# An attention and maxout kernel: first loads in another order, other first transposes, one store per output tile, score bursts of three

## The chip, the cores and the metric

The kernel runs on 1 core of one Trainium2 chip. The metric is device microseconds (us) of one execution, from the first instruction to the last. Several executions of each kernel are timed, and the median is quoted with all or with the lowest and highest. Two numbers are quoted per kernel: the timed median, and the "span" of its one profiled execution, which comes out about two microseconds shorter (before: 384.99 timed, 382.8 span).

## The reference

```python
# q, k, v: (8 batches, 8 heads, 1152, 64); w1, w2: (512, 1024); w_out: (1024, 512); all float32
q_pool = q.reshape(8, 8, 576, 2, 64).mean(axis=3)            # 576 pooled queries a head
attn   = softmax(q_pool @ k.T / sqrt(64))                    # 576 x 1152 a head
x      = (attn @ v).transpose(0, 2, 1, 3).reshape(4608, 512) # tokens x features
out    = maximum(x @ w1, x @ w2) @ w_out                     # (4608, 512)
```

The kernel computes the second half as relu(x(w1-w2)) w_out + x(w2 w_out). In the profile L582 (before) or L618 (after) is x(w1-w2), called h below; L609 (L645) is the last product, 12 matmuls of 128x512 for an output tile of 128 tokens, called p. In some variants these lines are one to six off.

## The kernel before

The program is put in order on the host, while it is built. `Plan.op` adds an instruction with the names that it reads and writes, and a planned cost. A loop picks what TensorE does next by these planned times; semaphores then keep the order safe whatever the true times are. So each engine runs a fixed list of instructions, and a new planned cost or rank reorders all lists. Work goes by pairs of heads (32 pairs): scores for two heads at once as two 64-row tiles of TensorE, exponentials on ScalarE (128x1024 each, 336 in all), the product with v (AV), and, once the 4 pairs of a batch are done, x is transposed and h and p run between the scores of the next batches. The score steps need another tiling of TensorE (64 rows) than all else (128 rows), so they come in bursts; a "switch" or "transition" below is a change between the two.

These parts matter (cuts marked):

```python
def load_k(i, lo=0, hi=NT):              # first K in two loads, three tiles and six
    ...
def load_q(i):                           # first queries in two loads, one head (64 partitions) each
    ...
def qtrans(i):                           # pooled queries of a pair: 9 transposes of 64 rows x 128 columns
    ...
def xtrans(b):                           # x of batches 1 to 6: five transposes by DMA, issued from SyncE
    ...
def store(lo, s):
    for half in range(2):                # a tile of 128 tokens: two stores of 64 rows
        n0 = lo + half * HP              # HP = 64, QU = 9, SQ = 576, HP * QU = SQ
        b, at = n0 // SQ, n0 % SQ
        if b % 2:
            at = (at - NB) % SQ
        op("SP", lambda e, b=b, u=at // HP, half=half: e.dma_start(
            out[b * SQ:(b + 1) * SQ, :].rearrange("(p u) e -> u p e", u=QU)[u, :, :],
            osb[s][rows(half), :]), r=[f"osb{s}"], dma=f"d_o{s}", cost=0.4)
...
def burst_size():
    done = [b for b in range(B) if ...]
    return 3 if len(done) * SQ - p_end[0] > LAG else 2
...
X_PE = (0, B - 1)                        # x of the first and last batch: transposed by TensorE
rank = {"q": 6, "k": 6, "x": 5, "a": 4, "w": 3, "p": 2, "h": 1}
```

Column n of a batch's queries inside the kernel is not row n of the output: the queries were loaded with 9 neighbouring rows to a partition, so block u of 64 columns holds the rows 0*9+u, 1*9+u, ..., 63*9+u. A tile of 128 tokens is two such blocks, u and u+1. In four tiles the two blocks belong to two neighbouring batches and have the same u. Each store writes 64 rows of 2048 bytes that lie 9 rows apart.

The softmax here doesn't subtract the row's maximum and nothing guards it: scores larger than these inputs give would overflow.

## Time and profile before

| | before |
|---|---|
| median of 3 runs | 384.99 us (383.74 to 385.46) |
| span of the profiled execution | 382.8 us |
| TensorE busy | 363.7 us, 95% |
| ScalarE busy | 316.9 us, 83% |
| first matmul of h, L582 | 65.85 us |
| end of the last matmul | 378.68 us |
| transitions between 64-row and 128-row work | 272, of which 204 after 65 us |

PE is TensorE at matmuls and PEld at weight loads, DVE is VectorE, ACT ScalarE, POOL GpSimd, and SPq the queue of DMAs that SyncE issues, one after the other. PEclk is the clock that TensorE was granted, in tenths of full speed.

The same execution by stretches: to the first matmul, to the first h, to the end of the last matmul, and the rest. The columns are given by the first line.

```profile
core 0: us, PE busy (x) PEld busy (x) DVE busy (x) ACT busy (x) POOL busy (x), PEclk, DMA share, GB/s
0.00:6.70 6.70, 0.00 (x0) 0.00 (x0) 1.50 (x2) 1.56 (x2) 0.97 (x10) 1.00 0.70 184
6.70:65.80 59.10, 51.75 (x837) 32.08 (x838) 31.03 (x58) 55.57 (x63) 40.05 (x30) 1.00 1.11 368
65.80:378.70 312.90, 311.95 (x4180) 178.76 (x4175) 107.00 (x222) 259.77 (x292) 120.96 (x96) 1.00 0.87 208
378.70:382.80 4.10, 0.00 (x0) 0.00 (x0) 0.69 (x1) 0.00 (x0) 0.00 (x0) 1.00 0.40 84
```

Two lines of the waits of this kernel, and three of SyncE's queue near 90 us, for comparison later. The waits give total us, times, and the longest. Names: qp and qpT are the pooled queries and their transpose, kbf and kT the same for K, xnat and xT for x; sps are the banks of memory into which TensorE writes scores (the score banks), fb its other banks.

```profile
PE fb L323 <- DVE qp L297: 6.7, 1, 6.7
POOL qp L297 <- DMA qpT<-qp: 21.3, 13, 4.3
```

```profile
88.33 3.81 SPq L286 DMA_TRANSPOSE kT<-kbf  x1
...
95.59 7.50 SPq L475 DMA_TRANSPOSE xT<-xnat  x5
103.19 1.94 SPq L336 DMA_TRANSPOSE qpT<-qp  x1
```

TensorE starts by waiting 6.7 us for the first pooled queries. The list of waits has no line of TensorE waiting for a DMA at all. GpSimd waits 21.3 us for transposes by DMA to free their source, without harm.

### The profile page before, as it was taken

Reading aid. Unit: us, or ns where it says so; the run is one execution under the profiler, and the core shown is the slowest. Engines: PE = TensorE matmul, PEld = TensorE weight load, DVE = VectorE, ACT = ScalarE, POOL = GpSimd, SP = SyncE. Lnnn points to the kernel's source line nnn. Section 1 sums busy time; section 2 is a strip of 40 time slices with the busy share of each in tenths; the row PEclk is TensorE's granted clock in tenths of the full one; section 3 lists DMA queues with packets and bytes.
Section 4 is the critical chain, followed back from the end, with each engine's and each line's share of the span. In section 5 each row is a group of like instructions: output and inputs, shape, how many; then the busy total and the mean of one; then the engine's idle time right before and its main releaser. Section 6 shows DMA issues by size and latency. Waiting matters only on the chain.

```text
span 382.8 us, 11318 instructions
## 1 busy us (share of the span) xinstructions
PE 363.7 (95%) x5010; PEld 210.8 (55%) x5010; DVE 140.2 (37%) x283; ACT 316.9 (83%) x355; POOL 162.0 (42%) x135
## 2 busy tenths in 40 slices
PE   2787999999999999999999999999999999999995
PEld 1365546555555555455556565555455655667642
DVE  2274934442234223422252224422442244237201
ACT  3998989999999999999999999999899999902210
POOL 1955597665554555555453535545545110000000
PEclk9999999999999999999999999999999999999999
DMA  8999999999989998999799999999899460121144
GB/s 248 405 391 399 392 257 312 331 309 312 225 234 295 273 272 174 309 320 275 142 265 289 319 179 212 286 258 315 200 236 267 94 109 14 29 44 42 29 95 98
DMA packets 93521, 88.58 MB, mean 231 GB/s; under 512 B 66080, under 2 KB 66592, under 8 KB 93472
## 3 DMA queue, kind: packets, MB, share of 16 engines
q1 hardware_dynamic: 93472, 87.86, 89.4%
q8 instruction: 39, 0.64, 0.7%
q14 instruction: 10, 0.08, 0.1%
HBM read 62.91 MB, written 9.44 MB: 189 GB/s over the span
## 4 chain that ended last, share of the span: by engine, by line
PE 85%; DMA 6%; DVE 4%; POOL 2%; issue 1%; SPq 1%; POOLq 0%
PE fb L378 22%; PE fb L609 21%; PE sps L429 18%; PE fb L582 15%; PE sps L609 4%; DMA qraw<-in_q_dram 3%; DMA kraw<-in_k_dram 2%; PE sps L582 2%; DVE wd L519 2%; POOL qp L297 1%; PE fb L547 1%; DVE xnat L390 1%; POOL vE L304 1%; PE fb L489 1%; DVE wo L523 1%
## 5 line engine op out<-in xcount | busy, mean ns | idle before, releaser
L436 ACT ACTIVATE et<-sps 128x1024 bf16<-128x1024 f32 (+1 forms) x336 | 307.8, 1005 | 19.0 <-PE sps L429 17.2
L378 PEld LDWEIGHTS fb<-vE,et 128*128 128x128 bf16 x2880 | 93.4, 97 | 20.9 <-issue 10.9
L378 PE MATMUL fb<-vE,et 128*128 128x65 bf16 x2880 | 101.9, 193 | 0.3
L297 POOL TENSOR_TENSOR qp<-qraw 64x576 bf16<-64x576 f32 x62 | 88.6, 1429 | 30.6 <-DMA qpT<-qp 21.3
L429 PE MATMUL sps<-qpT,kT 64*128 64x512 bf16 (+7 forms) x1152 | 96.9, 289 | 3.0 <-ACT et L436 2.1
L304 POOL TENSOR_SCALAR vE<-vraw 128x1152 bf16<-128x1152 f32 x32 | 36.9, 1152 | 103.2 <-PE fb L378 95.8
L429 PEld LDWEIGHTS sps<-qpT,kT 64*128 64x128 bf16 x1152 | 41.8, 95 | 51.3 <-issue 19.6
L582 PE MATMUL fb<-xT,wd 128*128 128x512 bf16 (+3 forms) x276 | 63.1, 360 | 0.7 <-DVE stage L623 0.7
L609 PE MATMUL fb<-wo,stage 128*128 128x512 bf16 x240 | 62.4, 380 | 0.0
L593 DVE TENSOR_SCALAR stage<-fb 128x512 bf16<-128x512 f32 (+3 forms) x64 | 41.9, 657 | 32.3 <-PE fb L582 32.1
L388 DVE RECIPROCAL rc<-fb 128x5 f32<-128x5 f32 x64 | 12.4, 194 | 112.3 <-PE fb L378 112.3
L273 POOL TENSOR_SCALAR kbf<-kraw 128x1152 bf16<-128x1152 f32 x31 | 36.2, 1167 | 14.6 <-DMA kraw<-in_k_dram 12.5
L582 PEld LDWEIGHTS fb<-xT,wd 128*128 128x128 bf16 x276 | 22.8, 98 | 29.4 <-DVE stage L593 6.3
L623 DVE COPY stage<-fb 128x512 f32<-128x512 f32 x29 | 20.0, 690 | 50.2 <-PE fb L609 49.7
L609 PEld LDWEIGHTS fb<-wo,stage 128*128 128x128 bf16 x240 | 21.1, 97 | 23.3 <-issue 3.3
L390 DVE TENSOR_TENSOR xnat<-fb,rc 128x320 bf16<-128x320 f32 x64 | 31.5, 491 | 2.2
L609 PE MATMUL fb<-w,xT 128*128 128x512 bf16 x120 | 32.1, 380 | 0.0
L609 PEld LDWEIGHTS fb<-w,xT 128*128 128x128 bf16 x120 | 10.3, 98 | 11.7 <-issue 2.0
L589 ACT ACTIVATE stage<-sps 128x256 bf16<-128x256 f32 (+1 forms) x7 | 2.3, 338 | 16.4 <-PE sps L582 16.4
L620 ACT COPY stage<-sps 128x512 f32<-128x512 f32 x3 | 1.8, 585 | 13.8 <-PE sps L609 13.8
L609 PE MATMUL sps<-wo,stage 128*128 128x512 bf16 x48 | 11.3, 379 | 0.0
L582 PE MATMUL sps<-xT,wd 128*128 128x256 bf16 (+2 forms) x76 | 10.3, 275 | 0.0
(40 smaller groups left out, 96.4 us busy)
## 6 DMA issues: line engine op xcount, KB each, us to landing
vraw<-in_v_dram SPq DMA_DIRECT2D x32, 576.0 KB, 7.7
kraw<-in_k_dram SPq DMA_DIRECT2D x31, 576.0 KB, 6.6
qraw<-in_q_dram SPq DMA_DIRECT2D x31, 576.0 KB, 5.8
out_dram<-stage SPq DMA_DIRECT2D x72, 128.0 KB, 2.4
xT<-in_moe_w_dram SPq DMA_DIRECT2D x4, 512.0 KB, 11.9
stage<-in_moe_w_out_dram SPq DMA_DIRECT2D x4, 512.0 KB, 14.2
stage<-in_moe_w_dram SPq DMA_DIRECT2D x4, 512.0 KB, 13.2
qraw<-in_q_dram SPq DMA_DIRECT2D x2, 288.0 KB, 4.1
```

The source lines that it names most:

```text
L273: op("POOL", lambda g: g.tensor_scalar(kbf[s][:, :, :, :].rearrange("p t h d -> p h t d"), kraw[r][:, :, :, :], 1.0, 1.0, ALU.mult, ALU.mu ...
L297: op("DVE" if i == 0 else "POOL", lambda g, half=half, a=a: g.tensor_tensor(qp[s][:, :, half, :], a[:, :, 0, :], a[:, :, 1, :], ALU.add), ...
L304: op("POOL", lambda g: g.tensor_scalar(vE[r][:, :, :, 0:D].rearrange("p t h d -> p h t d"), vraw[r][:, :, :, :], 1.0, 1.0, ALU.mult, ALU.m ...
L378: last = e.matmul(fb[m][:, sb * 66:sb * 66 + 65], et[:, a:a + P], vE[vs][:, t, half, 0:65], start=(t == 0), stop=(t == NT - 1))
L388: dve(lambda e: e.reciprocal(rc[half][:, :], a[:, :, 64:65]), [f"f{m}"], [f"rc{half}"], 0.19)
L390: dve(lambda e: e.tensor_tensor(xnat[xs][:, :, c:c + D], a[:, :, 0:D], rc[half][:, :].unsqueeze(2).to_broadcast([P, NCH + 1, D]), ALU.mult ...
L429: last = e.matmul(sps[r][:, h, col:col + hi - lo], kT[i % 3][rows(h), t, :], qpT[i % 3][rows(h), lo:hi], start=True, stop=True)
L436: op("ACT", lambda e: e.activation(et2[:, :, c:c + z - a], sps[r][:, :, a - g * W:z - g * W], EXP, scale=scale), r=[f"s{r}"], w=keys + [f" ...
L582: return e.matmul(fb[m][:, 0:size], wd[:, ct, ft * P:(ft + 1) * P], xT[:, ct, n0:n1], start=(ct == 0), stop=(ct == NC_ - 1))
L593: dve(lambda e: e.tensor_scalar_max(gT[:, ft, g0:g0 + size], fb[m][:, 0:size], 0.0), [f"f{m}"], w, 0.1 + size / 960.0)
L609: return e.matmul(fb[m][:, :], lhs, rhs, start=(j == 0), stop=(j == NC_ + NF - 1))
L623: dve(lambda e: e.tensor_copy(osb[o][:, :], fb[m][:, :]), [f"f{m}"], [f"osb{o}", f"f{m}"], 0.63)
```

## The change

The intent is to start earlier (loads and pooling), to make TensorE switch less between its tilings, to issue half as many stores, and to shorten the end. The diff is long; this is its core.

```diff
-        def load_k(i, lo=0, hi=NT):
+        def load_k(i):                     # first K: one load
...
-            for half in range(2) if i == 0 else (None,):
+            for lo, hi in zip(Q0, Q0[1:]) if i == 0 else ((0, QU),):   # Q0 = (0, 5, QU): two column parts
...
+        def cast_q0(i, lo, hi):            # pairs 0 and 1 pooled by VectorE on 128 partitions
+            op("DVE", lambda e: e.tensor_tensor(
+                qpf[i][:, lo:hi, :], qraw[i][:, lo:hi, 0, :], qraw[i][:, lo:hi, 1, :], ALU.add), ...
+        def qtrans0(i, lo, hi):            # and transposed as 64x64 blocks on two quadrants
+                for u in range(lo, hi):
+                    for h in range(2):
+                        last = e.transpose(
+                            mb[rows(h), (u - lo) * HP:(u - lo + 1) * HP],
+                            qpf[i][rows(h), u, :], ident[rows(h), rows(h)])
...
-        def store(lo, s):
-            for half in range(2):
-                ...
+        def store(lo, s, c0=0, c1=E, eng="SP"):
+            b, at = lo // SQ, lo % SQ
+            u = at // HP if b % 2 == 0 else (at - NB) // HP
+            if u == QU - 1:
+                to = out[b * SQ:(b + 2) * SQ, c0:c1].rearrange("(b p u) e -> u b p e", b=2, u=QU)[u]
+            else:
+                to = out[b * SQ:(b + 1) * SQ, c0:c1].rearrange("(p u) e -> u p e", u=QU)[u:u + 2]
+            op(eng, lambda e: e.dma_start(to, osb[s][:, c0:c1]), r=[f"osb{s}"],
+               dma=f"d_o{s}" if eng == "SP" else "d_z", cost=0.75 * (c1 - c0) / E)
...                                         # last tile in two parts, 384 and 128 columns:
+                    queue["p"].extend(p_job(p_at[0], tail, *c) for c in ((0, 384), (384, E)))
...
-            return 3 if len(done) * SQ - p_end[0] > LAG else 2
+            return 3 if done else 2
...
+        for kind, i in zip(*[iter("q2k2b2k3v1b0q3c0c3k4c2v2q4c1v3")] * 2):   # loads, weights among them
...
-        rank = {"q": 6, "k": 6, "x": 5, "a": 4, "w": 3, "p": 2, "h": 1}
+        rank = {"q": 6, "k": 6, "x": 5, "h": 5, "a": 4, "w": 3, "p": 1}
```

The cut parts: the first K is cast in three parts by ScalarE and GpSimd; planned costs, and the stall that the plan allows before a burst, are adjusted; VectorE waits for its own earlier results; the stores at the end are issued at once.

## The prediction

> **What bounds the kernel now.** The page's busy table has PE 95% and ACT 83% busy in a 382.8 us span; the chain that ended last is 85% PE. The spacing of the matmul records splits this up. The first matmul starts at 6.7 us. Until 65.8 us, where the first matmul of w1-w2 (L582) runs, PE has only about 46 us of work (scores, AV, transposes, w21), so about 13 us is idle: ACT sets the pace there. Its 128x1024 exponentials follow each other every 903 ns at best, and 58 groups took 56.5 us from 8.91 us, about 4 us over that pace; the stalls are at 11.6 (0.4), 34.2 (1.2, K of a later pair late through the POOL queue) and 48.5 us (0.9, PE waiting for VectorE). From 65.8 to 378.7 us PE is full: I count about 305 us of work, and little of the rest is waiting. In it are some 200 switches between the 64-row score tiles and 128-row work, 95 to 99 ns extra each. The Trainium skill ("TensorEngine Tiling (Array Packing)", Key Properties) says changing the tiling mode drains TensorE; these gaps agree. The tail is 4.1 us: 0.69 us eviction, two store issues of 0.55 us, 2.3 us to landing. The skill ("DMA: Bandwidth & Descriptors") gives about 2.0 us fixed cost; this agrees.
>
> **What the change does.**
> 1. Bursts of three: the static order has 126 score bursts instead of 132, so 252 switches instead of 264. About 1.2 us, mostly given back by extra small transposes. Net PE work 0.7 us less.
> 2. Early loads and VectorE pooling of the second pair. DMA moves about 400 GB/s until 45 us in the timeline, so only order changes. Walking the new order at that rate, each cast lands before its scores are due. The ACT stalls at 34 and 48 us should go, and the first h matmul moves from group 60 to group 59: about 62 us instead of 65.8. Gain 3.5 to 4 us, all on the critical path since PE is full afterwards.
> 3. Head: nearly nothing. K still lands at about 7.2 us (the same bytes lie ahead). One tile's cast is shorter (0.3 against 0.52 us), so the first exponential comes at 8.7 to 8.9 us. But VectorE's order puts pooling of the second pair's queries (0.75 us, waiting for a fourth load at about 8.6 us) ahead of the copies of the remaining K transposes, so I expect a stall of about 0.6 us before the second exponential.
> 4. Tail: the last tile split 384+128 with one store each: eviction 0.3 instead of 0.69, one issue instead of two. About 0.95 us.
> 5. h ahead of p, and the two mixed: fewer 88 ns waits for a PSUM bank. 0.5 us.
> Half as many stores, and waits of VectorE on itself: off the critical path.
>
> **Prediction.** 385.0 - 3.8 (early phase) - 1.0 (tail) - 0.7 (switches, bank waits) = 379.5 us; 376.5 to 382.5 holds it 8 in 10. Faster by over 2%: 0.2; within 2%: 0.78; slower: 0.02.
>
> **What would show it.** First h matmul near 62 us; exponentials at 903 to 920 ns spacing from 11 to 60 us; a gap before the second exponential ended by VectorE; PE last matmul to span end about 3.1 us; PE idle smaller almost only before 65 us; ACT's last exponential several us before 335 us.
>
> **What would make it wrong.** Loads landing more than 2 us later than I walked, which stalls scores in program order; bursts of three faster than ACT empties the banks, which turns switches into waits on exponentials in the middle; PE waits on transposes by DMA under the new order.

## More of the kernel before

The page of the kernel before: the busy table, rows of the 40 slices (one digit is the busy share of a fortieth of the span, in tenths), the chain of work that ended last, and the row of the output stores in the table of DMA issues (count, size, time from issue to landing).

```profile
span 382.8 us, 11318 instructions
PE 363.7 (95%) x5010; PEld 210.8 (55%) x5010; DVE 140.2 (37%) x283; ACT 316.9 (83%) x355; POOL 162.0 (42%) x135
...
PE   2787999999999999999999999999999999999995
...
PEclk9999999999999999999999999999999999999999
DMA  8999999999989998999799999999899460121144
...
PE 85%; DMA 6%; DVE 4%; POOL 2%; issue 1%; SPq 1%; POOLq 0%
...
out_dram<-stage SPq DMA_DIRECT2D x72, 128.0 KB, 2.4
```

TensorE is full from the fifth slice to the end, its clock is granted in full, and it makes 85% of the chain. Note the DMA row too: the 16 DMA engines are nearly always busy until the last fifth. The 72 stores land 2.4 us after issue.

In the third stretch TensorE is busy for 311.95 of 312.90 us. What is left to gain is in the first two stretches and the last, or in TensorE's work itself. And 0.87 is the DMA share of that third stretch: the DMA engines are little of a spare resource there. (The share adds up the times of the packets, which can overlap: it is 1.11 in the second stretch. So it is a rough measure.)

## The result, and the profile after

| | before | after |
|---|---|---|
| median | 385.02 us (4 runs) | 457.79 us; runs 1234.92, 458.83, 455.62, 456.76 |
| ratio, fast runs | | 1.187 (1.180 to 1.193) |

Ratios here and below are the mean time of one kernel's fast runs over that of the other's of the same rounds, so not quite the ratio of the medians quoted; the range is the 95% interval.

A gain of 1.4% was predicted; the kernel became 19% slower. One execution of four, the profiled one, was far slower still. Two different things have to be kept apart, so both pages follow. First the page of the slow execution:

```profile
span 1233.2 us, 11290 instructions
PE 1183.9 (96%) x4982; PEld 555.3 (45%) x5040; DVE 147.8 (12%) x284; ACT 322.4 (26%) x358; POOL 160.8 (13%) x134
...
L618 PE MATMUL fb<-xT,wd 128*128 128x512 bf16 (+3 forms) x274 | 204.9, 973 | 7.4 <-issue 7.4
```

TensorE is busy for 1183.9 us with as many matmuls as ever; the others' busy times are nearly as before. In the trace, matmuls of 512 columns follow each other 840 ns apart (216 ns before) from 10.7 us to the end. TensorE ran at about a quarter of its rate. The record has no event of a granted clock at all for this execution, and the clock is listed as 1.0. This is a state, not the kernel's normal time, so the same kernel was run again unaltered (after_again below): 456.75 us. Its page is the one to compare with before:

```profile
span 454.9 us, 11290 instructions
PE 373.8 (82%) x4982; PEld 216.5 (48%) x5040; DVE 140.8 (31%) x284; ACT 317.2 (70%) x358; POOL 161.3 (35%) x134
...
PE   4989999993997799883997999857994999999900
...
PEclk9999999997998989995998999996997999999965
DMA  8999899998997997999998999998998520011111
...
PE 41%; DMA 22%; ACT 14%; SPq 10%; POOL 4%; issue 3%; DVE 2%; POOLq 0%; ACTq 0%
...
out_dram<-stage SPq DMA_DIRECT2D x35, 256.0 KB
```

Its stretches, with the same columns as before:

```profile
0.00:61.90 61.90, 51.34 (x821) 31.98 (x827) 34.28 (x63) 54.43 (x62) 36.39 (x36) 1.00 0.95 337
61.90:107.00 45.10, 40.89 (x608) 24.03 (x615) 13.70 (x29) 43.14 (x48) 27.26 (x22) 1.00 1.23 289
107.00:432.00 325.00, 281.55 (x3553) 160.44 (x3598) 92.12 (x191) 219.06 (x248) 97.62 (x77) 0.94 0.87 165
432.00:454.90 22.90, 0.00 (x0) 0.00 (x0) 0.69 (x1) 0.59 (x1) 0.00 (x0) 0.57 0.13 49
```

And lines of its waits:

```profile
POOL qp L315 <- DMA qpT<-qp: 123.0, 20, 13.2
...
PE fb L618 <- DMA xT<-xnat: 23.9, 4, 8.4
...
ACT stage L674 <- DMA out_dram<-stage: 14.3, 1, 14.3
```

What the reader is to see:

- Up to the first h the change did what was predicted: 61.9 us against 65.85. ScalarE's idle times of 1.03 and 0.82 us that end at 36.35 and 50.31 us in before are gone, and 59 exponentials start before the first h instead of 61.
- In the third stretch TensorE is busy for 281.55 of 325 us, where it was full before. What it waits for is transposes by DMA: 23.9 us for xT and 9.3 us for kT directly, and through GpSimd, whose wait for DMA transposes grew from 21.3 to 123.0 us, for later pairs' queries and keys.
- The last stretch, 4.1 us before, is 22.9 us, and in it nothing computes but two evictions. Its last two columns are the clue: the DMA share is 0.13, and 2 of 16 engines are 0.125; they move 49 GB/s.
- The row of the stores has no landing time. The page derives it from the count of 16 on a semaphore, and the stores did not count that way (next paragraph).
- The granted clock is 0.94 in the third stretch. In the trace each of the seven half-rate pieces there begins during an idle stretch of TensorE of 2.4 to 8.4 us or less than 2 us after it (TensorE stands from 103.6 to 110.7 us, and one piece lasts from 107.7 to 114.6), so we read it as a consequence of the waits.

The trace records each arrival at a semaphore. In before, 72 stores make 1152 arrivals, 16 each; loads and transposes make 16 each, in all kernels. In after_again, 37 stores (36 tiles, one of them in two parts) make 163. That is 33 x 3 + 4 x 16. The four with 16 are the tiles that lie in two batches, whose access pattern is 128 rows at one step; the other 33 have a pattern of 2 blocks x 64 rows. The Trainium skill ("DMA: Bandwidth & Descriptors", section "Why a DMA increments its semaphore by 16 and not by 1") says how many engines a DMA uses: the largest number up to 16 that divides the slowest dimension, other than 1, of both access patterns; only those engines count on the semaphore, and the issuing sequencer writes the rest. Three arrivals, two engines and the sequencer's one, are what it says for a slowest dimension of 2. This trace agrees.

So the theory: the slice `[u:u+2]` puts a dimension of size 2 outermost, each such store runs on 2 engines of 16, and everything else that needs all 16 engines waits behind them there. The size fits, as an estimate: the stores' packets of 2048 bytes took 84 ns (median, in before_1store below), and 32 such stores x 64 packets an engine x 84 ns are 172 us on each of the two engines. Spread over 16 engines, all 4608 packets are 24 us an engine. With a DMA share of 0.87 in before's third stretch, taken as even over the engines, each has some 40 us to spare (0.13 x 313), not the 150 us more that two of them would need.

The rivals were these. The first came first: the 1233 us suggested that the new 64x64 transposes of the first queries on two quadrants (Q in the texts), or their being the first work of TensorE, bring about a slow TensorE. The second: a store of 256 KB, or one DMA for a tile, is itself the trouble, whatever its engines. The third: the new order, with its ranks and bursts, costs it.

### The profile page after: what moved, and what is told of

Same layout as the page of the kernel before. It is cut to its first block, busy times and chain, and to the rows that moved or that the text cites. A ratio compares the mean times of both kernels' runs of the same rounds, so it can differ in the third digit from the quotient of the medians.

```text
span 1233.2 us, 11290 instructions
## 1 busy us (share of the span) xinstructions
PE 1183.9 (96%) x4982; PEld 555.3 (45%) x5040; DVE 147.8 (12%) x284; ACT 322.4 (26%) x358; POOL 160.8 (13%) x134
## 4 chain that ended last, share of the span: by engine, by line
PE 94%; issue 3%; another core or an unknown queue 1%; DMA 1%; DVE 0%; ACTq 0%; ACT 0%; SPq 0%
PE fb L414 24%; PE sps L467 22%; PE fb L645 21%; PE fb L618 16%; PE sps L645 4%; PE sps L618 2%; PE fb L584 2%; PE fb L384 1%; DMA kraw<-in_k_dram 1%; PE fb L568 1%; PE sps L414 0%; PE fb L526 0%; PE sps L526 0%; PE fb L341 0%
## 5 line engine op out<-in xcount | busy, mean ns | idle before, releaser
L414 PEld LDWEIGHTS fb<-vE,et 128*128 128x128 bf16 x2835 | 294.4, 169 | 70.2 <-issue 60.3
L414 PE MATMUL fb<-vE,et 128*128 128x65 bf16 x2835 | 309.9, 335 | 0.0
L467 PE MATMUL sps<-qpT,kT 64*128 64x512 bf16 (+7 forms) x1152 | 278.1, 691 | 1.9 <-issue 1.5
L618 PE MATMUL fb<-xT,wd 128*128 128x512 bf16 (+3 forms) x274 | 204.9, 973 | 7.4 <-issue 7.4
L645 PE MATMUL fb<-wo,stage 128*128 128x512 bf16 (+1 forms) x202 | 182.6, 1079 | 15.5 <-issue 15.5
L467 PEld LDWEIGHTS sps<-qpT,kT 64*128 64x128 bf16 x1152 | 83.4, 159 | 209.3 <-issue 201.3
L618 PEld LDWEIGHTS fb<-xT,wd 128*128 128x128 bf16 x288 | 51.5, 189 | 133.9 <-issue 120.1
L645 PE MATMUL fb<-w,xT 128*128 128x512 bf16 (+1 forms) x109 | 97.0, 1090 | 3.1 <-issue 1.9
L645 PE MATMUL sps<-wo,stage 128*128 128x512 bf16 (+1 forms) x63 | 49.0, 1036 | 0.7 <-issue 0.7
L618 PE MATMUL sps<-xT,wd 128*128 128x384 bf16 (+3 forms) x64 | 33.2, 767 | 0.5 <-issue 0.5
```

What stands on the lines that cost most here:

```text
L414: last = e.matmul(fb[m][:, sb * 66:sb * 66 + 65], et[:, a:a + P], vE[vs][:, t, half, 0:65], start=(t == 0), stop=(t == NT - 1))
L467: last = e.matmul(sps[r][:, h, col:col + hi - lo], kT[i % 3][rows(h), t, :], qpT[i % 3][rows(h), lo:hi], start=True, stop=True)
L618: return e.matmul(fb[m][:, 0:size], wd[:, ct, ft * P:(ft + 1) * P], xT[:, ct, n0:n1], start=(ct == 0), stop=(ct == NC_ - 1))
L645: return e.matmul(fb[m][:, 0:c1 - c0], lhs, rhs[:, c0:c1], start=(j == 0), stop=(j == NC_ + NF - 1))
```

## The experiments

Two to four kernels at a time ran on one chip, beside runs of the kernel before there ("before" in the tables). Variants of after are named after_..., of before before_..., and s2_... are after with two stores. The letters of theories in the texts are new in each round (Q in s2_rank's is not the Q of the first). Where the order of TensorE's instructions is said to be the same, that was compared instruction by instruction.

### First round: is it the first transposes?

**after_again**: the changed kernel, unaltered.

> The changed kernel, unaltered, to see whether its slowness repeats on this chip and to have a profile of its usual state. Its first profile (1233 us) shows 128-column transposes 210 ns apart and 512-column matmuls 840 ns apart from the start to the end, against 56 and 216 ns in the kernel before: TensorE runs at about a quarter of its rate all the time and no clock event is recorded. Theory Q (the new 64-row x 64-column query transposes, first work of TensorE, put the clock into a throttled state): about 457 us again, part of the run at the quarter rate, granted clock under 1. Theory D (the denser schedule, bursts of three and h before p[...]): about 457 us, with the low rate in the dense middle, not at the start. Theory I (TensorE starts at 4.7 us, then idles 3.8 us until K[...]): about 457 us, slow from the start. Theory C (chance, this chip only): near 380 us in some rounds.

**after_q128**: after, but the first two pairs' queries transposed as before, 64 rows x 128 columns. TensorE's order of work is the same.

```diff
-                    for h in range(2):
-                        last = e.transpose(mb[rows(h), ...], qpf[i][rows(h), u, :], ident[rows(h), rows(h)])
+                    last = e.transpose(mb[:, ...], qp[i][:, u, :, :].rearrange("p h d -> p (h d)"), ident[0:HP, 0:HP])
```

> The changed kernel with one thing undone: the queries of the first two pairs are transposed as 64 rows x 128 columns, as before (VectorE pools each part in two instructions, one for each head, onto 64 partitions). Loads, order on TensorE and everything else are the same; the order is identical apart from the shape of these 36 transposes. Theory Q: 377 to 383 us, clock as in the kernel before (128-column transposes 107 ns apart at first, 56 ns after some 10 us). Theories D and I: still about 457 us, since density and the early start with the idle stretch are unchanged.

**before_q64**: before, with the change's 64x64 transposes for the first two pairs (the opposite edit).

> The kernel before with only the transposes of the queries of its first two pairs made 64 x 64 (two heads on two quadrants, 18 instead of 9 instructions); the order on TensorE is otherwise identical. Theory Q: over 440 us, perhaps 1200 in some runs, low rate from the start. Theories D and I: 384 to 387 us.

**after_warm**: after, with 32 transposes of the 128x128 identity as TensorE's first work.

```diff
+        op("PE", warm, r=["ident"], w=["s2"], ...)    # 32 transposes of ident into an unused score bank
```

> The changed kernel with 32 transposes of the identity, 128 x 128, put before its first query transposes, so that TensorE does not start with 64 x 64 work; it still idles until K lands. Theory Q in the form that 64 x 64 work is bad only as the first work on a cold array: about 380 us. Theory Q in the form that any 64 x 64 work is bad (the second pair has 18 more at 13.7 us): about 457 us or more. Theory I: about 457 us, since the idle stretch from 5.5 to 8.8 us is still there. Theory D: about 457 us.

| run | all runs, us | before, us | ratio |
|---|---|---|---|
| after_again | 455.88 to 458.79 | 384.54 | 1.189 (1.185 to 1.193) |
| after_q128 | 900.3, 460.15, 460.35, 457.01 | 384.54 | 1.194 (1.189 to 1.199) |
| before_q64 | 383.86 to 384.78 | 384.54 | 1.000 (0.998 to 1.001) |
| after_warm | 454.28 to 456.62 | 384.54 | 1.185 (1.182 to 1.188) |

The rival of the first transposes is dead: without those transposes the loss stays, with them before keeps its time, and other first work changes nothing. The slow state came once more, in after_q128, which has no such transposes (898.6 us span, matmuls of 512 columns 621 ns apart, and again no event of a granted clock).

### Second round: the store alone, on an unchanged order

**after_2stores**: after, with only the two 64-row stores back. TensorE's order is the same.

```diff
-            (one DMA with the pattern [u:u + 2])
+            for half in range(2):
+                ...
+                    out[b * SQ:(b + 1) * SQ, c0:c1].rearrange("(p u) e -> u p e", u=QU)[u, :, :],
+                    osb[s][rows(half), c0:c1]), ...
```

> The profile of the changed kernel's usual state (455 us) shows TensorE waiting for DMA transposes of x, q and k between 110 and 350 us, and stores that end 20 us after the last matmul. Theory S: the store of a whole output tile is written as a pattern of 2 x 64 rows, so it runs on only two of the 16 DMA engines (the Trainium skill, DMA: Bandwidth & Descriptors, says the number is the largest one up to 16 that divides the slowest dimension of both sides); at 256 KB a store those two fall behind, and every load and transpose, which needs all 16, waits for them. This run undoes only that: two stores of 64 rows a tile, as before, the order on TensorE identical. Theory S: 376 to 383 us, last matmul to the end about 3.5 us, no TensorE waits on DMA transposes. Rival R (the early loads and the new order of h and p ask for transposes before they can be done, whatever the stores): still over 440 us.

**before_1store**: before, with only the change's store. TensorE's order is the same.

> The kernel before with only its stores changed to one a tile as in the change (2 x 64 rows), held back as before; the order on TensorE identical. Theory S: well over 385, about 430 to 480 us, with the same waits on DMA transposes. Rival R: 384 to 387 us.

**after_rows**: after, with one store of 256 KB to 128 neighbouring rows. The rows of the output are in the wrong order.

```diff
-            (one DMA with the pattern [u:u + 2])
+            op(eng, lambda e: e.dma_start(out[lo:lo + P, c0:c1], osb[s][:, c0:c1]), ...
```

> The changed kernel with one store of a whole tile, 256 KB as in the change, but to 128 neighbouring rows of the output instead of 2 x 64 interleaved ones, so that both sides have 128 as their slowest dimension. The rows land in the wrong order, so the result is wrong on purpose. Theory S (two engines): 376 to 383 us. Theory S2 (it is the size, one 256 KB store against two of 128 KB, that blocks others): still over 440 us. Rival R: over 440 us.

| run | median (all), us | before, us | ratio | arrivals a store |
|---|---|---|---|---|
| after_2stores | 387.82 (386.77 to 388.06) | 384.15 | 1.009 (1.007 to 1.010) | 16 |
| before_1store | 460.29 (457.68 to 461.72) | 384.15 | 1.197 (1.193 to 1.202) | 3 (32 stores), 16 (4 stores) |
| after_rows | 386.52 (386.09 to 387.46) | 384.15 | 1.007 (1.005 to 1.009) | 16 |

Theory S had the direction and the end of the loss right, but after_2stores missed its 376 to 383 us and its "no TensorE waits on DMA transposes"; that is the third round. The page and the waits of before_1store:

```profile
span 457.6 us, 11282 instructions
...
out_dram<-stage SPq DMA_DIRECT2D x36, 256.0 KB
```

```profile
POOL qp L297 <- DMA qpT<-qp: 117.1, 20, 13.9
...
PE fb L581 <- DMA xT<-xnat: 38.0, 6, 12.4
```

And of after_2stores:

```profile
POOL qp L315 <- DMA qpT<-qp: 30.0, 17, 5.2
...
PE fb L619 <- DMA xT<-xnat: 3.7, 1, 3.7
```

And of after_rows, where the stores have a landing time again:

```profile
span 384.4 us, 11348 instructions
...
out_dram<-stage SPq DMA_DIRECT2D x35, 256.0 KB, 2.7
```

```profile
POOL qp L315 <- DMA qpT<-qp: 11.8, 5, 5.1
...
PE fb L612 <- DMA xT<-xnat: 3.9, 1, 3.9
```

The store alone makes the loss appear in before, with the same waits on transposes, and go from after. With that the denser order and the early start (theories D and I of the first round, rival R here) are out as causes: after_2stores keeps both. The rival of one big DMA is dead too: one DMA of the same 256 KB that uses 16 engines does no harm (after_rows; it is 0.2% nearer to before than after_2stores). What differs between after and after_rows is the pattern on the side of the output, and with it the number of engines. That the rows are interleaved is not the trouble: in after_2stores they are too. That it is two engines is read from the arrivals and from the DMA share of 0.13; the trace does not name the engine of a packet. after_rows was not flagged as wrong by the comparison with the reference: its tolerance is too wide for outputs this small. That the other variants are right rests on their patterns, which are those of before or of the change.

The time of 457 us splits like this (span of the profiled execution; "rest" is from the first h to the end of the last matmul, "tail" from there to the end):

| | first h | rest | tail | span |
|---|---|---|---|---|
| before | 65.85 | 312.8 | 4.15 | 382.8 |
| before_1store | 65.95 | 368.8 | 22.9 | 457.6 |
| after_again | 61.91 | 369.3 | 23.7 | 454.9 |
| after_2stores | 63.07 | 318.0 | 3.96 | 385.0 |

The tail shows the mechanism bare. There TensorE makes a tile each 2.6 us (12 x 0.216), and a store on two engines takes 64 x 84 ns = 5.4 us, an estimate from the packets. The stores fall behind, the four buffers fill, and the last eviction waits 14.29 us for a store to free its buffer, as this line of after_again shows:

```profile
440.38 0.59 ACT L674 COPY stage<-sps 128x512 f32<-128x512 f32 x1 [14.29 <-DMA out_dram<-stage]
```

### Third round: why is after_2stores still no faster than before?

With the store repaired the rest of the change should have given 5 us, by the prediction. The table says where they are: 2.8 us gained before the first h, 0.2 in the tail, and 5.2 lost between. In the middle TensorE stops at 105 us:

```profile
108.70 1.02 PE L619 MATMUL fb<-xT,wd 128*128 128x512 bf16 x4 [3.70 <-DMA xT<-xnat]
```

and again at 147.7 us, for 1.4 us: x of a batch is not there yet. SyncE's queue of after_2stores near 90 us, beside that of before shown earlier:

```profile
89.28 6.86 SPq L298 DMA_TRANSPOSE kT<-kbf  x1
...
99.26 7.82 SPq L512 DMA_TRANSPOSE xT<-xnat  x5
```

Normalised x of the second batch is ready at 93.7 us (before: 95.0), but its transposes are issued from 99.26 us (before: 95.59), because SyncE stands at an earlier transpose of K until 96.1 us (before: 92.1) and then issues three loads and two stores. The last of the five lands at 108.6 us (before: 106.1), and TensorE goes on at 108.7. We take it that the order of SyncE's list decides; no run moved these issues alone.

Such a wait can cost more than its length. In the profiles of s2_tail and s2_rank (below) the clock is at half rate for 6.83 us from 106.67 us and for 3.41 us from 107.53 us, in and after this wait. The profiled execution of after_2stores has no such piece; with 386.77 us and a mean clock of 0.998 it is the fastest of the four, and the two at 0.991 took 387.97 and 388.06.

There are four theories. Ranks: h ahead of p pulls h early onto an x that is not there. Head: VectorE's pooling of the second pair's queries before the copies of K costs the start. Tail: the split tile is not the last in the planned order. SyncE's order: the transposes of x stand behind its other work. Each is an edit to after_2stores.

```diff
# s2_rank:  rank = {..., "x": 5, "a": 4, "w": 3, "p": 2, "h": 1}                 as before
# s2_q1:    later("qraw1", lambda: (cast_q0(1, 0, QU), ...), margin=1.5)         pooling behind K's copies
# s2_tail:  cand.append((t, -rank[job.kind], len(job.units) + late, kk))         late = 200 + c0 for the last tile
# s2_all:   all three
# s2_xpe:   X_PE = (0, 1, B - 1)                                                 x of batch 1 transposed by TensorE
# s2_all_xpe: all four
```

> With two stores a tile the changed kernel still took 387.8 us against 384.2. Its first h matmul is 2.8 us earlier than before (63.1 against 65.9 us), but TensorE then waits 3.9 us at 105 us and 1.4 us at 148 us for the DMA transposes of x of the second and third batch. This run is that kernel with the ranks of before (p ahead of h). Theory H (h ahead of p reaches the next batch sooner than its transposes can land): these waits go, 381.5 to 383.5 us. Theory Q (the transposes are late because SyncE, in order, is held up by a transpose of k that waits for the casts; the order of h and p does not matter): still a wait of over 2 us near 105 us, 385 to 388 us.

> Two stores a tile, and the pooling of the second pair's queries put behind the copies of the first K transposes on VectorE. Measured without it: the second exponential starts 1.0 us late, after VectorE has pooled queries that landed at 9.0 us. If that stall counts: second exponential 0.9 us after the first, first h matmul 0.7 to 1.0 us earlier (62.2 us), and the time 0.5 to 1 us less (386.8 to 387.3). If the time of the x transposes decides what comes after: the stall goes and the wait at 105 us grows by as much, 387.3 to 388.3 us.

> Two stores a tile, and the tile that is split in 384 and 128 columns made the last one that TensorE works on (in the change two whole tiles come after it, so the end waits for a 128 x 512 eviction and its stores as before: 3.95 us from the last matmul to the end). If the split tail was worth what I predicted, last matmul to the end falls to 3.0 to 3.3 us and the time by 0.7 to 1 us (386.8 to 387.2). If the end is set by something else, no change.

> All three together. If the three reasons are right and add up: 380 to 382 us, about 1% faster than the kernel before and what the prediction meant. If only ranks matter: 381.5 to 383.5 us.

> Two stores a tile, and x of the second batch transposed by TensorE instead of by DMA (the code has a list of batches for this: 0 and the last; here also 1). In the kernel with two stores TensorE waits 3.9 us at 105 us for those DMA transposes: x is normalised at 93.7 us, but SyncE issues them only from 99.3 to 107.1 us, behind a transpose of k that occupies it until 96.1 us (92.1 in the kernel before). If the order of SyncE's issues is the cause: the wait at 105 us goes, the cost is about 1.2 us of TensorE work and the time falls by 2 to 3 us, to 384.5 to 386 us. If TensorE is short of work there for another reason (nothing else it could do until x is there): the wait moves elsewhere, 387 to 388.5 us.

> The best version so far (two stores, p ahead of h, queries of the second pair pooled later, split tile last; 384.0 us) with the second batch of x transposed by TensorE too. It still waited 1.3 us at 105 us; less 1.3, plus 1.2 us of TensorE work: 383 to 384.5 us. If it gains 1 us or more the wait cost more than its own length.

| run | median (all), us | before, us | ratio |
|---|---|---|---|
| s2_rank | 386.00 (385.18 to 386.77) | 384.87 | 1.002 (1.000 to 1.004) |
| s2_q1 | 385.25 (383.32 to 387.19) | 384.87 | 1.001 (0.998 to 1.004) |
| s2_tail | 386.78 (386.02 to 387.21) | 384.87 | 1.004 (1.002 to 1.006) |
| s2_all | 383.98 (381.99 to 384.81) | 384.87 | 0.996 (0.994 to 0.999) |
| s2_xpe | 384.85 (384.57 to 385.29) | 384.58 | 1.000 (0.998 to 1.003) |
| s2_all_xpe | 383.81 (383.32 to 385.00) | 384.58 | 0.997 (0.994 to 1.000) |

- Ranks: theory H failed by its own figures (waits gone, at most 383.5 us), and the outcome is what theory Q of that text said: with the old ranks some time returns (1.002 against 1.009), but the wait at 105 us is still 2.49 us.
- Head is not shown, and neither of its expectations was met (385.25 us, below both). In after_2stores the second exponential starts 1.91 us after the first (0.92 before), and pooling does stand between, as the lines below show. In s2_q1 pooling comes later, and the distance is 1.51 us; but it is 1.51 us also in s2_rank, s2_tail, s2_xpe and after_rows, where pooling is still ahead. In these K landed later, and pooling no longer held up the scores: they start 0.86 us after the first exponential in s2_tail as in s2_q1, against 1.26 us in after_2stores. So pooling costs up to 0.4 us, and the rest of the distance is not its doing. When K lands differs between executions of the same loads: ScalarE's first cast of K starts at 6.23 us in after_again, 7.16 in after_2stores and 7.86 in s2_q1 (before: 6.42). From that cast to the first h it is 55.7, 55.9 and 55.3 us (before: 59.4). So the 2.8 us of after_2stores against the 3.9 of after_again is mostly when K landed, and s2_q1's first h at 63.18 us, no earlier than 63.07, hides a gain of 0.6 us at most. Its time fell for another reason as well: its wait for x is 1.82 us.
- Tail is half right: the time fell within the range expected (386.78 us), the tail less than that. The planned order puts the two parts of the split tile ahead of two whole tiles, so the execution still ends with a whole eviction and its stores. Put last, from the last matmul to the end takes 3.5 us, against 3.96 and before's 4.15. The two stores a tile, put back here, cost the rest: in after_rows, with one store and a whole last eviction, it is 3.07 us.
- All three together missed: 383.98 us, where 380 to 382 was expected if the reasons add up. s2_all_xpe came out where expected (383.81 us).
- SyncE's order is supported, not isolated: with x of the second batch transposed by TensorE, no wait of TensorE over 0.4 us is left after 60 us, and the span falls from 385.0 to 382.9 us, with 1.2 us more TensorE work for the transposes (expected: 384.5 to 386 us timed; measured 384.85). So x's transposes by DMA were the wait. Whether their late issue or their own time, the run does not tell.
- What remains in the middle of s2_xpe (316.4 us against 312.8) is mostly that extra work and waits between scores of one burst, about 3.4 us more than in before: a burst of three catches up with the exponentials and waits 0.14 to 0.28 us for a score bank. That is shown by the trace only; no run undid the bursts alone.

The only line that the list of TensorE's waits has for s2_xpe from 60 to 380 us (the short waits inside bursts do not show in it):

```profile
PE fb L619 <- DVE stage L630: 0.4, 2, 0.2
```

The start in after_2stores (from its timeline; in brackets, idle time before and what ended it):

```profile
8.84 1.02 ACT L474 ACTIVATE et<-sps 128x1024 bf16<-128x1024 f32 x1 [1.07 <-PE sps L467]
9.08 0.76 DVE L306 TENSOR_TENSOR qp<-qraw 128x576 bf16<-128x576 f32 x1 [0.95 <-DMA qraw<-in_q_dram]
9.76 0.75 DVE L391 COPY kT<-fb 128x256 bf16<-128x256 bf16 x2
...
10.75 2.86 ACT L474 ACTIVATE et<-sps 128x1024 bf16<-128x1024 f32 x3 [0.88 <-PE sps L467]
```

VectorE pools from 9.08 us, copies K from 9.76, and only then come the scores that release the second exponential at 10.75 us. The same exponential in s2_q1 (pooling later; the first starts at 9.55 us) and in s2_tail (pooling still ahead; 9.12 us):

```profile
11.06 2.85 ACT L474 ACTIVATE et<-sps 128x1024 bf16<-128x1024 f32 x3 [0.48 <-PE sps L467]
```

```profile
10.63 2.85 ACT L474 ACTIVATE et<-sps 128x1024 bf16<-128x1024 f32 x3 [0.48 <-PE sps L467]
```

The end in after_2stores and in s2_tail:

```profile
381.09 0.58 ACT L675 COPY stage<-sps 128x512 f32<-128x512 f32 x1 [5.37 <-PE sps L646]
```

```profile
381.73 0.29 DVE L663 COPY stage<-sps 128x128 f32<-128x128 f32 x1 [4.52 <-PE sps L646]
```

The best versions, s2_all and s2_all_xpe, are 0.3 to 0.4% faster than before. Their intervals exclude equality by little.

What stays open: the slow state of 1233 and 900 us. It fell on 2 of 20 executions of kernels with stores on two engines (after, after_again, after_q128, after_warm, before_1store), both times the first of its kernel on the chip, which is the profiled one, and on none of the others. Two of 20 is too few to lay it to the store. Why SyncE stood 6.86 us at one transpose of K is not settled either.

## Why the prediction was wrong, point by point

- **The step that failed** is the sentence "Half as many stores, and waits of VectorE on itself: off the critical path." The prediction counted stores and their issues, and did not ask how many engines each store runs on. The skill's rule, in the very page that the prediction cited for the fixed cost, would have told (the fixed cost is there a fit to DMAs that GpSimd issues; these stores are SyncE's, and the 2.3 us of the trace decide): the pattern `[u:u + 2]` has a slowest dimension of 2. The stores then delayed what TensorE needs: before waited for no DMA transpose, before_1store 38.0 us for those of x. Measured: 384 to 460 us when the store alone changes (before_1store), and 457 to 388 us when it alone is undone (after_2stores).
- **The early phase** was right in mechanism and nearly in size: 3.5 to 4 us predicted, "about 62 us" for the first h; 3.9 us and 61.91 in after_again, 2.8 us and 63.07 in after_2stores, where K landed 0.9 us later. The stalls of ScalarE named for 34 and 48 us went. That K would land at "about 7.2 us" was not safe: its first cast starts between 6.0 and 8.4 us in the kernels with the new loads.
- **The head**: a stall of about 0.6 us before the second exponential, ended through VectorE. The stall came, 1.12 us idle in after_again and 0.88 in after_2stores. But pooling is only a part of it: 0.48 us stays in s2_q1.
- **The sentence "all on the critical path since PE is full afterwards"** failed as well. Of the 2.8 us nothing was left at the end of after_2stores: TensorE was ready for the second batch's h at 105 us, and x's transposes landed 2.5 us later than before. The prediction had named this as a danger ("PE waits on transposes by DMA under the new order"), but put no size to it; it was 3.7 and 1.4 us.
- **The tail**: 1.0 us predicted (0.39 of it a smaller eviction, the rest one store issue instead of two), 0.2 measured in after_2stores, which has two stores again and does not end with the split tile. The order was there to be read before. Put last, the split gives 0.6 with two stores. In after_rows one store alone gives 1.1 (3.07 against 4.15 us): the predicted size, but without the smaller eviction.
- **Switches and bank waits**, 0.7 us predicted: the transitions fell about as counted, from 204 to 191 after 65 us in after_2stores, at 95 to 99 ns extra each, about 1.2 us (a matmul of 512 columns is followed by another after 216 ns, by a score after 312). The waits inside bursts rose by more than that; this too was named as a danger and not sized.
- **"Slower: 0.02"** was far too sure for a change with a new access pattern in it.

## What to carry to other kernels

When two DMAs are merged into one, look at the slowest dimension of both access patterns: a leading 2 makes a DMA on two engines, and where the DMA engines are busy, as here, that can delay everything that needs all 16. The arrivals on its semaphore, a missing landing time and a DMA share of 2/16 in a quiet stretch give it away. And a gain ahead of a full engine counts only if what that engine needs next comes earlier as well: here x's transposes by DMA, issued 5.5 us after x was ready, landed later than before.

## What the Trainium skill lacked or had wrong

- "DMA: Bandwidth & Descriptors", "Rules for kernel authors": the row on two transfers to disjoint partition halves says to use one 128-partition transfer instead. Done as in this change, that took before from 384.15 to 460.29 us. The row "Use all 16 engines" further down says why, but the two rows don't point to each other, and the merged one needs the condition that the other side's pattern stays one dimension of 128. Where it does, after_rows does not contradict the row: 386.52 us with one store, 387.82 with two (ratios to before 1.007 and 1.009, whose intervals overlap).
- The same page, "Why a DMA increments its semaphore by 16 and not by 1": right here (3 arrivals a store on two engines, 16 on all). It has no measurement of what DMAs on few engines do to the others: GpSimd's waits for DMA transposes grew from 21.3 to 117.1 us in before_1store.
- "TensorE: Matmul & The Clock Gate", Part 1, speaks of a clock stuck at a quarter for 50 us and more. Here whole executions were slow, 1233.2 and 898.6 us, with no clock event in either record, and the spacing of 512-column matmuls was 840 ns in one and 621 ns in the other, against 216; the second is not a quarter.
- "TensorEngine Tiling (Array Packing)", Key Properties, says that a change of tiling mode drains TensorE, without a figure. Here each switch cost 95 to 99 ns extra.
